# Retention scores from unscaled queries and keys, a block ahead, before two feed-forward layers

## Chip, cores, metric

One core of a Trainium2 chip. The metric is device time in microseconds (us) of one execution, the median of several runs. The engines are TensorE (PE, the matrix multiplies; PEld is its loading of weights), VectorE (DVE), ScalarE (ACT), GpSimd (POOL) and SyncE (SP), which here issues all transfers.

## What is computed

```python
scores = scale * np.matmul(q, k.transpose(0, 1, 3, 2))
gamma = 1.0 - 2.0 ** (-5.0 - np.arange(H, dtype=np.float32))
rel = pos[:, None] - pos[None, :]
Dmat = np.where(rel >= 0, gamma[:, None, None] ** rel[None, :, :], 0.0)
ret = np.matmul(scores * Dmat[None, :, :, :], v)
x = ret.transpose(0, 2, 1, 3).reshape(B * S, H * D)
h = x @ w_in;  x = (h * sigmoid(h)) @ w_out
h = x @ w2_in; y = (np.maximum(h, 0.0) + alpha * np.minimum(h, 0.0)) @ w2_out
```

B = 4 sequences, H = 8 heads, S = 576 positions, D = 64; 2304 tokens in all, model width 512, inner width 2048. Everything is float32.

## The kernel before

**Stages.** The tokens are 18 blocks of 128. Retention is computed block by block in chunks of 64 positions (two chunks to a block, nine to a sequence): scores between the positions of one chunk, and a running state (keys times values of the chunks before) for everything earlier. Its results, split into a high and a low part (`xhi`, `xlo`), feed the two feed-forward layers. Those run over five token tiles (256, then four of 512) and over groups of the inner width; each product is three matmuls (high times high, low times high, high times low). The weights come as 512 KB transfers into `raw` and are decoded into a high and a low part by ACT, DVE and POOL (`weight`).

**A retention block.** Each block's q, k (features in partitions) and k, v (tokens in partitions) come as two transfers of 512 KB into a pack of four slots (`att_load`): slots 0 and 1 are q and k for the scores, slots 2 and 3 are k and v for the state and the output. There are five packs, two of them in the still unused end of `sums`. `att_prep` multiplies q by a table of decay factors (`qtab`, built piece by piece by `att_table`) and v by another one, in place, on POOL or on DVE. `att_half`, called twice a block, alternates on PE eight score products (into the buffer `sc`) and eight state products (into `total`), all 64x64, and copies the state. `att_mask` multiplies the scores by a mask of ones and zeros: the decay is already in q and v. `att_out` makes the products of old state and q and of masked scores and v in the buffer `xo`, and copies out `xhi` and `xlo`. There is one `sc`, one `total` and one `xo`.

**What sets the order.** All instructions are recorded first and then ordered by a planner (`Program.order`): every engine but PE takes the ready instruction with the earliest due time; on PE there are two queues of units, "retention" and "layers", and a started unit is finished first. `DUE` gives the first two weights due times of their own. On each engine, and in SP's queue of transfers, the order that comes out is kept as it stands: an instruction that waits holds up those behind it. In `att_step(n)` block n+1 is loaded, scaled and scored while block n's output is made. Some transfers wait for a one-column copy on ACT (`gate`) that stands for an earlier transfer or result.

**Start.** 22 matmuls on a zero tile (`warm(WARM)`) run while the first data comes; the first six blocks have two more each, so 34 in all.

Names in the rows: `sums` (two packs and later the layers' sums), `pack_111` to `pack_113` (the other packs), `att` (score and state tiles, tables, masked scores), `bank` (accumulators of the layers), `low`, `top`, `a`, `w` (weight decoding). Nearly every instruction is recorded by one helper, so it carries line 280 (281 in the changed kernel).

Of the kernel before, what the change touches and what calls it, by code (L numbers as in the profile page):

```python
# [9 lines left out]
F32 = mybir.dt.float32  # L10
# [8 lines left out]
P = 128  # L19
# [7 lines left out]
C = 64  # L27
# [3 lines left out]
SIZES = [[1, 2, 3, 4, 4, 2], [4, 4, 4, 4]]  # L31
GROUPS = [(i, range(sum(sizes[:n]), sum(sizes[:n + 1]))) for i, sizes in enumerate(SIZES) for n in range(len(sizes))]
WARM, WARM_BLOCKS = 22, 6
DUE = {0: -1e5, 1: 6e3}
LATER = [5, 6, 8, 9, 11, 12]
LEAD = 4
TILES = [256, 512, 512, 512, 512]
RAWS = 2
PACKS = 5
STATES = 4  # L40
PERIOD = 2 * S // P
SMALL = [C, PERIOD * H, NPAIR * NCH, NPAIR * C]
ORDER = [0, 2, 4, 6, 1, 3, 5, 7]


# [238 lines left out]
def retention_ffn_kernel(ctx: ExitStack, tc: tile.TileContext, qkv, w1, w2, alpha, small, out):  # L284
# [37 lines left out]
            self.n += 1  # L322
            return self.tiles[(self.n - 1) % len(self.tiles)]

    rings = {k: Ring() for k in ("w0", "w1", "g", "act", "down", "pr", "state", "bank", "raw", "top", "low", "a")}
    rings["raw"].grow(big, "raw", 512, RAWS, I64)
    rings["top"].grow(big, "top", 512, 2)
    rings["low"].grow(big, "low", 512, 2)
# [12 lines left out]
    att = att_pool.enter_context(tc.tile_pool(name="att", bufs=1))  # L341
    PACK = 4 * DM
    spare = [sums[:, NC * NT - (i + 1) * PACK:NC * NT - i * PACK] for i in range(2)]
    packs = [att.tile([P, PACK], F32, name=f"pack{i}") for i in range(3)]
    packs = [spare[0], packs[0], packs[1], spare[1], packs[2]]
    sizes = 2 * [2 * NPAIR * C] + STATES * [NPAIR * D] + SMALL + [NPAIR * S]
    ends = np.cumsum([0] + sizes)
    rest = att.tile([P, int(ends[-1])], F32, name="att")
    *more, mask, vtab, fac, base, qtab = (rest[:, a:b] for a, b in zip(ends, ends[1:]))
    small_sb = rest[:, ends[-6]:ends[-2]]  # L350
    mask = mask.unsqueeze(1).unsqueeze(1).to_broadcast([P, 2, NPAIR, C])
    vtab = vtab.rearrange("p (n h) -> p n h", h=H)
    fac = fac.rearrange("p (c n) -> p c n", c=NPAIR)
    base = base.rearrange("p (c t) -> p c t", c=NPAIR)
    qtab = qtab.rearrange("p (c n t) -> p c n t", c=NPAIR, t=C)
    rings["pr"].tiles = more[:2]
    rings["state"].tiles = more[2:]

    def close_att():
        nc.issue()  # L360
# [7 lines left out]
    def pack(n):  # L368
        return packs[n % PACKS].rearrange("p (s a) -> p s a", s=4)

# [55 lines left out]

    probs, states = {}, {}

    def rows(j):
        return slice(j * C, (j + 1) * C)

    def quarter(out, lhsT, rhs, start=True):
        nc.tensor.matmul(out, lhsT, rhs, start=start, stop=True, skip_group_check=True)

    def heads(n, i):
        return pack(n)[:, i].rearrange("p (h d) -> p h d", h=H)

    def pairs(n, i):  # L440
        return pack(n)[:, i].rearrange("p (c t) -> p c t", c=NPAIR)

    def att_load(n):
        if 0 < n < PACKS:
            for i in (0, 2):
                gate(pack(n)[:, i], fac[:, 0] if n == 1 else pack(n - 2)[:, i + 1])
        nc.sync.dma_start(out=pack(n)[:, 0:2], in_=qkv[n, :, 0:2])
        nc.sync.dma_start(out=pack(n)[:, 2:4], in_=qkv[n, :, 2:4])
# [5 lines left out]
    def att_prep(n):  # L454

        prep = ("gpsimd", "tensor_tensor"), ("vector", "tensor_tensor")
        q = pack(n)[:, 0].rearrange("p (c x t) -> p c x t", x=2, t=C)
        at = 2 * n % NCH
        for a, b, x in ((at, at + 2, 0),) if at + 2 <= NCH else ((at, NCH, 0), (0, 1, 1)):
            if 2 * n < NCH and a:  # L460
                att_table(a, b)
            part = q[:, :, x:x + b - a]
            nc.either(prep, out=part, in0=part, in1=qtab[:, :, a:b], op=ALU.mult)
        v = heads(n, 3)
        nc.either(prep, out=v, in0=v, in1=vtab[:, n % PERIOD].unsqueeze(2).to_broadcast([P, H, D]), op=ALU.mult)

    def att_half(n, c):

        nc.unit("retention", c == 1)
        q, k = pairs(n, 0), pairs(n, 1)  # L470
        j = 1 - c
        g = 2 * n + c
        more = (g + 1) % NCH
        k2, v2 = heads(n, 2)[rows(c)], heads(n, 3)[rows(c)]
        for p in range(NPAIR):
            for i in range(2):
                quarter(two["sc"][rows(i), j, p * C:(p + 1) * C], k[rows(j), p, rows(i)], q[rows(j), p, rows(i)])
                if more:
                    quarter(total[rows(i), p * D:(p + 1) * D], k2[:, 2 * p + i], v2[:, 2 * p + i],
                            start=g % NCH == 0 and p == 0)  # L480
        if more:
            states[g + 1] = rings["state"].next()
            nc.either(COPY, states[g + 1], total[:, 0:NPAIR * D])

    def att_mask(n):
        probs[n] = rings["pr"].next()
        nc.vector.tensor_tensor(out=probs[n].rearrange("p (j c t) -> p j c t", j=2, c=NPAIR),
                                in0=two["sc"][:, :, 0:NPAIR * C].rearrange("p j (c t) -> p j c t", c=NPAIR),
                                in1=mask, op=ALU.mult)

    def att_out(n):


        at = n * P
        t0, tn = next((a, m) for a, m in SPANS if a <= at < a + m)
        q, v = pairs(n, 0), heads(n, 3)
        xo = two["xo"][:, :, 0:2 * P]
        pr = probs.pop(n).rearrange("p (j c t) -> p j c t", j=2, c=NPAIR)
        hi, lo = (acts(x, t0, tn)[:, :, at - t0:at - t0 + P] for x in (xhi, xlo))
        begun = set()  # L500

        def mm(j, p, c, lhsT, rhs):
            half = p % 2
            quarter(xo[rows(half), j, p // 2 * P + c * C:p // 2 * P + (c + 1) * C], lhsT, rhs,
                    start=(j, half) not in begun)
            begun.add((j, half))

        nc.unit("retention", True)
        for c in range(2):
            g = 2 * n + c  # L510
            if g % NCH:
                old = states[g].rearrange("p (c d) -> p c d", c=NPAIR)
                for p0 in range(0, NPAIR, 2):
                    for j in range(2):
                        for p in (p0, p0 + 1):
                            mm(j, p, c, old[rows(j), p], q[rows(j), p, rows(c)])

        def inside(cross):
            for p0 in range(0, NPAIR, 2):
                for c in range(2):  # L520
                    j = c ^ cross
                    for p in (p0, p0 + 1):
                        mm(j, p, c, v[rows(c), 2 * p + j], pr[rows(c), j, p])

        def copy(cross):
            a, b = xo[:, :, cross * C:], hi[:, :, cross * C:]
            step = (C, -C)[cross]
            nc.either(COPY, bass.AP(tensor=b.tensor, offset=b.offset, ap=[b.ap[0], (2 * tn + step, 2), (tn, 2), (1, C)]),
                           bass.AP(tensor=a.tensor, offset=a.offset, ap=[a.ap[0], (512 + step, 2), (P, 2), (1, C)]))

        inside(0)
        copy(0)
        yield
        nc.unit("retention", True)
        inside(1)
        copy(1)
        nc.vector.tensor_tensor(out=lo.rearrange("p (j p2) t -> p j p2 t", j=2),
                                in0=xo.rearrange("p j (p2 t) -> p j p2 t", p2=2),
                                in1=f32(hi).rearrange("p (j p2) t -> p j p2 t", j=2), op=ALU.subtract)

    def att_step(n):

        m = n + 1
        out = att_out(n) if n >= 0 else iter([None])
        if m < NBLK:
            att_load(m)
            att_prep(m)
            att_half(m, 0)
            if m < WARM_BLOCKS:
                warm(1)  # L550
        next(out)
        if m < NBLK:
            att_half(m, 1)
            if m < WARM_BLOCKS:
                warm(1)
            att_mask(m)
        for _ in out:
            pass

# [89 lines left out]
    ctx.enter_context(tc.manual_schedule())  # L649
    nc.vector.memset(nalpha_sb, 0.0)  # L650
    nc.scalar.activation(nalpha_sb, nalpha_sb, AF.Sigmoid)
    nc.sync.dma_start(out=small_sb, in_=small)
    att_table(0, 2)

# [14 lines left out]
    nc.scalar.copy(zero, rings["act"].tiles[0])  # L669
    nc.unit("retention")  # L670
    warm(WARM)
    att_step(-1)
    first = [(s, u) for s in range(len(TILES)) for u in hs[s] + ys[s]]
    at = 0
# [25 lines left out]
def _tables():  # L700
    gamma = 1.0 - 2.0 ** (-5.0 - np.arange(H))
    scale = 1.0 / np.sqrt(D)
    mid = S // 2
    pairs = gamma.reshape(NPAIR, 2)
    i = np.arange(C)
    rel = i[None, :] - i[:, None]
    mask = np.tile(rel >= 0, (2, 1))
    place = (np.arange(P)[:, None] + P * np.arange(PERIOD)[None, :]) % S
    vtab = (gamma[None, None, :] ** (mid - place)[:, :, None].astype(float)).reshape(P, -1)
    mine = np.repeat(pairs.T, D, axis=0)  # L710
    fac = (mine[:, :, None] ** (C * np.arange(float(NCH)))[None, None, :]).reshape(P, -1)
    base = (scale * mine[:, :, None] ** (i - float(mid))[None, None, :]).reshape(P, -1)
    tables = [np.pad(a, ((0, 0), (0, n - a.shape[1]))) for a, n in zip((mask, vtab, fac, base), SMALL)]
    return np.ascontiguousarray(np.concatenate(tables, axis=1), dtype=np.float32)
# [40 lines left out]
```

## Time and profile before

| | us |
|---|---|
| median of 3 runs | 880.76 |
| lowest and highest | 879.07, 882.34 |
| the profiled execution | 881.32 |
| its span in the trace | 879.5 |

Times in the trace count from the span's start. A row of a timeline gives start and duration of an instruction (or of several merged ones, xN) and in brackets how long its engine had been idle before it and what released it; "issue" there means that the profile shows nothing that released it. A small 64x64 matmul leaves two records on PE, one of 128x512 leaves one.

### The profile page before, as it was taken

The page shows a single profiled execution, that of the slowest core. Times are in us where ns is not written, and L with a number is a line of the kernel's source. Part 1 is how long each engine was busy: PE and PEld are TensorE (multiplying, and loading weights), DVE is VectorE, ACT ScalarE, POOL GpSimd, SP SyncE. Part 2 cuts the span into 40 slices and gives each one's busy share as a digit, 9 for nine tenths or more (in the row PEclk, how much of TensorE's full clock was granted, in tenths as well). Part 3 has the DMA queues.
Part 4 walks back from the last instruction along what each step waited for, and adds up shares of the span by engine and source line. Part 5 has one row for each costly group of instructions (what it writes and reads, how often), then busy time and mean ns, then how long its engine had stood idle before and what let it go on. Part 6 is the DMA issues. An engine that isn't in the chain of part 4 may idle for free.

```text
span 879.5 us, 14420 instructions
## 1 busy us (share of the span) xinstructions
PE 855.5 (97%) x5966; PEld 715.1 (81%) x5966; DVE 560.7 (64%) x882; ACT 380.7 (43%) x720; POOL 129.2 (15%) x99
## 2 busy tenths in 40 slices
PE   7888999999999999999999999999999999999998
PEld 5666788888888888888888888888888888888887
DVE  5667589975943499536998622984369733954342
ACT  3345465453432255223556544763345533533340
POOL 3455121220200022101210100220003200200000
PEclk8899999999999999999999999999999999999999
DMA  7786042220200033101311000330012100101102
GB/s 272 248 275 230 3 144 74 71 72 24 97 1 1 1 96 100 44 1 48 96 49 45 4 1 1 97 97 0 1 48 97 49 0 1 49 1 48 49 25 96
DMA packets 17491, 58.32 MB, mean 66 GB/s; under 512 B 2064, under 2 KB 2448, under 8 KB 17424
## 3 DMA queue, kind: packets, MB, share of 16 engines
q1 hardware_dynamic: 17424, 57.38, 19.6%
q8 instruction: 47, 0.77, 0.3%
q14 instruction: 20, 0.16, 0.1%
HBM read 52.66 MB, written 4.72 MB: 65 GB/s over the span
## 4 chain that ended last, share of the span: by engine, by line
PE 91%; DVE 5%; issue 2%; DMA 1%; POOL 1%; SPq 0%; ACT 0%; POOLq 0%; DVEq 0%; ACTq 0%
PE bank L280 87%; PE xo L280 2%; DVE a L280 2%; PE sc L280 1%; PE total L280 1%; DMA sums<-in_qkv 1%; DVE act L280 1%; DMA pack<-in_qkv 1%; DVE att L280 0%; POOL sums L280 0%; DVE xlo L280 0%; POOL pack L280 0%; DVE top L280 0%; DVE gb L280 0%; DVE w L280 0%
## 5 line engine op out<-in xcount | busy, mean ns | idle before, releaser
L280 PE MATMUL bank<-xhi,w 128*128 128x512 f32 (+1 forms) x880 | 250.8, 370 | 0.0
L280 PEld LDWEIGHTS bank<-xhi,w 128*128 128x128 f32 x880 | 159.7, 189 | 28.1
L280 POOL TENSOR_TENSOR low<-low,top 128x512 f32<-128x512 f32 x64 | 92.9, 1458 | 595.8 <-DVE top L280 584.8
L280 DVE TENSOR_TENSOR sums<-bank,sums 128x512 f32<-128x512 f32 (+1 forms) x155 | 100.7, 651 | 98.1 <-PE bank L280 96.2
L280 PE MATMUL bank<-xlo,w 128*128 128x512 f32 (+1 forms) x440 | 162.2, 369 | 0.0
L280 ACT ACTIVATE act<-bank 128x512 f32<-128x512 f32 (+1 forms) x160 | 88.4, 553 | 122.1 <-PE bank L280 119.4
L280 PE MATMUL bank<-xhi,w0b 128*128 128x512 f32 (+1 forms) x400 | 113.2, 368 | 0.0
L280 DVE SCALAR_TENSOR_TENSOR act<-down,nalpha_sb,act 128x512 f32<-128x512 f32 (+1 forms) x80 | 58.7, 734 | 84.9 <-ACT act L280 84.3
L280 PEld LDWEIGHTS bank<-xlo,w 128*128 128x128 f32 x440 | 83.2, 189 | 13.8
L280 ACT ACTIVATE down<-bank 128x512 f32<-128x512 f32 (+1 forms) x80 | 44.4, 555 | 106.7 <-PE bank L280 106.0
L280 PEld LDWEIGHTS bank<-xhi,w0b 128*128 128x128 f32 x400 | 72.6, 189 | 12.6
L280 DVE TENSOR_TENSOR act<-bank,act 128x512 f32<-128x512 f32 (+1 forms) x80 | 50.8, 635 | 48.5 <-ACT act L280 48.4
L280 PE MATMUL bank<-xlo,w0b 128*128 128x512 f32 (+1 forms) x200 | 73.6, 368 | 0.0
L280 PE MATMUL bank<-gb,w1b 128*128 128x512 f32 (+1 forms) x292 | 67.1, 363 | 1.0 <-DVE act L280 1.0
L280 DVE TENSOR_TENSOR gb<-act,gb 128x512 fp32r<-128x512 f32 (+1 forms) x79 | 52.1, 662 | 22.8 <-ACT gb L280 22.6
L280 ACT CAST g<-act 128x512 fp32r<-128x512 f32 (+1 forms) x82 | 47.6, 581 | 39.6 <-DVE act L280 39.4
L280 PE MATMUL bank<-g,w 128*128 128x512 f32 (+1 forms) x268 | 64.4, 370 | 0.0
L280 PE MATMUL bank<-w1b,gb 128*128 128x512 f32 (+1 forms) x268 | 61.9, 380 | 0.2 <-DVE gb L280 0.2
L280 ACT CAST gb<-act 128x512 fp32r<-128x512 f32 (+1 forms) x79 | 45.2, 574 | 38.3 <-DVE act L280 38.2
L280 ACT ACTIVATE top<-raw 128x512 f32<-128x512 f32 x64 | 43.1, 674 | 41.6 <-POOL low L280 34.1
L280 PEld LDWEIGHTS bank<-gb,w1b 128*128 128x128 f32 x292 | 50.6, 189 | 9.8 <-DVE act L280 1.2
L280 PEld LDWEIGHTS bank<-w1b,gb 128*128 128x128 f32 x268 | 48.6, 188 | 10.1 <-DVE gb L280 0.6
(75 smaller groups left out, 1199.0 us busy)
## 6 DMA issues: line engine op xcount, KB each, us to landing
raw<-in_w SPq DMA_DIRECT2D x64, 512.0 KB, 3.6
pack<-in_qkv SPq DMA_DIRECT2D x22, 512.0 KB, 5.3
sums<-in_qkv SPq DMA_DIRECT2D x14, 512.0 KB, 4.4
out<-sums SPq DMA_DIRECT2D x17, 256.0 KB, 2.0
out<-sums SPq DMA_DIRECT2D x2, 128.0 KB, 1.7
att<-in_small SPq DMA_DIRECT2D x1, 214.0 KB, 3.7
alpha_sb<-in_alpha SPq DMA_DIRECT2D x1, 8.0 KB, 5.3
```

Source lines behind the costliest of these rows:

```text
L280: getattr(getattr(self.nc, name), method)(*args, **kwargs)
```

## The change

Scores are made from q and k as loaded. The decay within a chunk goes into the mask, which becomes a stored table of 512 columns (`SMALL` grows by 448 columns), so the score path needs no scaling. k in slot 2 is scaled in place of v, for the state alone; scaled q goes to a tile of its own (two of them) and serves the products with the state. `att_half` of block n now makes the scores of block n+1 beside the state of block n, so before the first block there is a call for its scores alone, with n = -1. Loads run a block earlier in the program (`att_load(m + 1)`), and block 0's is recorded first of all. There are four packs instead of five, three tiles of masked scores instead of two, and no due times of their own for the first two weights.

```diff
-DUE = {0: -1e5, 1: 6e3}
+DUE = {}
-PACKS = 5
+PACKS = 4
+QS = 2
-SMALL = [C, PERIOD * H, NPAIR * NCH, NPAIR * C]
+SMALL = [2 * NPAIR * C, PERIOD * H, NPAIR * NCH, NPAIR * C]
...
-    packs = [spare[0], packs[0], packs[1], spare[1], packs[2]]
-    sizes = 2 * [2 * NPAIR * C] + STATES * [NPAIR * D] + SMALL + [NPAIR * S]
+    packs = [spare[0], packs[0], spare[1], packs[1]]
+    sizes = (3 + QS) * [2 * NPAIR * C] + STATES * [NPAIR * D] + SMALL + [NPAIR * S]
...
-    mask = mask.unsqueeze(1).unsqueeze(1).to_broadcast([P, 2, NPAIR, C])
+    mask = mask.rearrange("p (j c t) -> p j c t", j=2, c=NPAIR)
...
     def att_prep(n):
+        k = heads(n, 2)
+        nc.either(prep, out=k, in0=k, in1=vtab[:, n % PERIOD].unsqueeze(2).to_broadcast([P, H, D]), op=ALU.mult)
         q = pack(n)[:, 0].rearrange("p (c x t) -> p c x t", x=2, t=C)
+        scaled[n] = rings["q"].next().rearrange("p (c t) -> p c t", c=NPAIR)
+        new = scaled[n].rearrange("p c (x t) -> p c x t", x=2)
...
-            part = q[:, :, x:x + b - a]
-            nc.either(prep, out=part, in0=part, in1=qtab[:, :, a:b], op=ALU.mult)
-        v = heads(n, 3)
-        nc.either(prep, out=v, in0=v, in1=vtab[:, n % PERIOD].unsqueeze(2).to_broadcast([P, H, D]), op=ALU.mult)
+            nc.either(prep, out=new[:, :, x:x + b - a], in0=q[:, :, x:x + b - a], in1=qtab[:, :, a:b], op=ALU.mult)
...
     def att_half(n, c):
...
-        more = (g + 1) % NCH
-        k2, v2 = heads(n, 2)[rows(c)], heads(n, 3)[rows(c)]
+        more = n >= 0 and (g + 1) % NCH
         for p in range(NPAIR):
             for i in range(2):
-                quarter(two["sc"][rows(i), j, p * C:(p + 1) * C], k[rows(j), p, rows(i)], q[rows(j), p, rows(i)])
+                if n + 1 < NBLK:
+                    q, k = pairs(n + 1, 0), pairs(n + 1, 1)
+                    quarter(two["sc"][rows(i), j, p * C:(p + 1) * C], k[rows(j), p, rows(i)], q[rows(j), p, rows(i)])
                 if more:
...
-        q, v = pairs(n, 0), heads(n, 3)
+        q, v = scaled.pop(n), heads(n, 3)
...
     def att_step(n):
...
-            att_load(m)
             att_prep(m)
+            if m + 1 < NBLK:
+                att_load(m + 1)
             att_half(m, 0)
...
-            att_mask(m)
+            if m + 1 < NBLK:
+                att_mask(m + 1)
...
+    att_load(0)
     nc.sync.dma_start(out=small_sb, in_=small)
...
     warm(WARM)
+    att_half(-1, 0)
+    att_half(-1, 1)
+    att_mask(0)
     att_step(-1)
...
-    mask = np.tile(rel >= 0, (2, 1))
+    decay = gamma[None, None, :] ** np.maximum(rel, 0)[:, :, None] * (scale * (rel >= 0))[:, :, None]
+    mask = np.tile(decay.reshape(C, C, NPAIR, 2).transpose(0, 3, 2, 1).reshape(C, -1), (2, 1))
```

The planner makes more of it than these lines tell. Three places in the built programs, each before and then after the change:

SP's queue at its start (`att<-in_small` is the table, `sums<-in_qkv` the two halves of block 0 and later of others, `raw` a weight):

```order
1 L280 DMA raw_69<-in_w 128x512
2 L280 DMA att<-in_small 128x428
3 L280 DMA sums<-in_qkv 128x1024 x2
4 L280 DMA pack_111<-in_qkv 128x1024 x2
5 L280 DMA pack_112<-in_qkv 128x1024 x2
6 L280 DMA sums<-in_qkv 128x1024 x2
```

```order
1 L281 DMA att<-in_small 128x876
2 L281 DMA sums<-in_qkv 128x1024 x2
3 L281 DMA raw_69<-in_w 128x512
4 L281 DMA pack_111<-in_qkv 128x1024 x2
5 L281 DMA sums<-in_qkv 128x1024 x3
6 L281 DMA pack_112<-in_qkv 128x1024
7 L281 DMA pack_111<-in_qkv 128x1024
8 L281 DMA pack_112<-in_qkv 128x1024
9 L281 DMA raw_70<-in_w 128x512
```

The first weight went from first to behind block 0, and from the fifth row on the halves of different blocks are mixed.

DVE's queue at its start (`att<-sc,att` is the mask multiply of a block, `att<-att` a piece of the decay table, `a`, `top`, `w` the first weight's steps, `w_1<-a,low` the last of them, which needs POOL's `low`):

```order
2 L280 TENSOR_TENSOR att<-att 128x4x128
3 L280 TENSOR_SCALAR a_75<-top_71 128x512
4 L280 SCALAR_TENSOR_TENSOR a_75<-top_71,a_75 128x512
5 L280 TENSOR_SCALAR top_71<-a_75 128x512
6 L280 TENSOR_TENSOR a_75<-a_75,w_0_77 128x512
7 L280 TENSOR_TENSOR att<-att 128x4x128
8 L280 TENSOR_TENSOR w_1_78<-a_75,low_73 128x512
9 L280 TENSOR_TENSOR pack_111<-pack_111,att 128x512
10 L280 TENSOR_TENSOR att<-sc,att 128x512
```

```order
2 L281 TENSOR_TENSOR att<-att 128x4x128
3 L281 TENSOR_TENSOR att<-sums,att 128x512
4 L281 TENSOR_TENSOR att<-att 128x4x128
5 L281 TENSOR_TENSOR att<-sc,att 128x512
6 L281 TENSOR_SCALAR a_75<-top_71 128x512
7 L281 SCALAR_TENSOR_TENSOR a_75<-top_71,a_75 128x512
8 L281 TENSOR_SCALAR top_71<-a_75 128x512
9 L281 TENSOR_TENSOR att<-att 128x4x128
10 L281 TENSOR_TENSOR att<-sc,att 128x512
```

PE's order where retention ends (`xo` products are a block's output, `total` and `sc` state and scores, `bank` layer 1):

```order
662 L280 MATMUL xo<-att,pack_111 64x64 x8
663 L280 MATMUL sc<-pack_112 64x64 x8
664 L280 MATMUL xo<-att,pack_111 64x64 x8
665 L280 MATMUL xo<-pack_112,att 64x64 x16
666 L280 MATMUL xo<-att,pack_112 64x64 x8
667 L280 MATMUL bank_103<-g_99,w_0_85 128x512
668 L280 MATMUL bank_103<-g_99,w_1_86 128x512
669 L280 MATMUL bank_103<-g_93,w_0_85 128x512
670 L280 MATMUL xo<-att,pack_112 64x64 x8
671 L280 MATMUL bank_104<-g_99,w_0_85 128x512
```

```order
648 L281 MATMUL xo<-att,sums 64x64 x8
649 L281 MATMUL bank_103<-g_99,w_0_85 128x512
650 L281 MATMUL bank_103<-g_99,w_1_86 128x512
651 L281 MATMUL bank_103<-g_93,w_0_85 128x512
652 L281 MATMUL xo<-att,sums 64x64 x8
653 L281 MATMUL bank_104<-g_99,w_0_85 128x512
654 L281 MATMUL bank_104<-g_99,w_1_86 128x512
655 L281 MATMUL bank_104<-g_93,w_0_85 128x512
656 L281 MATMUL bank_102<-g_99,w_0_85 128x512
657 L281 MATMUL bank_102<-g_99,w_1_86 128x512
658 L281 MATMUL bank_102<-g_93,w_0_85 128x512
659 L281 MATMUL xo<-att 64x64 x16
```

Before, the outputs of the last two blocks stood next to each other; now six matmuls of layer 1 stand between them, and one pack name fewer occurs.

## Rows read from the trace of the kernel before

**Rows 1.** The page: busy time of each engine (share of the span), instructions
```profile
PE 855.5 (97%) x5966; PEld 715.1 (81%) x5966; DVE 560.7 (64%) x882; ACT 380.7 (43%) x720; POOL 129.2 (15%) x99
```

**Rows 2.** Busy time by stretch: PE, PEld, DVE, ACT, POOL, then clock, DMA share, GB/s
```profile
0.00:16.10 16.10, 9.83 (x88) 7.15 (x89) 7.91 (x11) 5.46 (x15) 6.37 (x9) 0.91 0.78 260
16.10:33.80 17.70, 14.80 (x378) 11.64 (x379) 8.58 (x14) 4.65 (x14) 5.33 (x5) 0.69 0.79 281
33.80:104.40 70.60, 60.71 (x1842) 48.33 (x1842) 49.63 (x78) 35.30 (x83) 32.70 (x27) 0.98 0.56 190
104.40:879.50 775.10, 770.15 (x3662) 647.96 (x3660) 494.61 (x781) 335.27 (x609) 84.81 (x58) 1.00 0.14 46
```

**Rows 3.** PE's waits from 0 to 105 us: total, times, longest
```profile
PE total L280 <- issue: 7.1, 7, 2.6
PE sc L280 <- issue: 4.2, 4, 2.2
PE xo L280 <- DVE xlo L280: 2.8, 4, 1.3
```

**Rows 4.** PE's timeline, single places between 0 and 104 us
```profile
2.80 6.99 PE L280 MATMUL bank<-g 128*128 128x512 f32 x22 [2.80 <-ACT g L280]
...
11.41 0.27 PE L280 MATMUL total<-sums 64*64 64x64 f32 x1 [1.13 <-POOL sums L280]
...
12.03 0.49 PE L280 MATMUL bank<-g 128*128 128x512 f32 x1
...
16.11 0.33 PE L280 MATMUL sc<-pack 64*64 64x64 f32 x1 [2.19 <-issue]
...
17.29 0.79 PE L280 MATMUL bank<-g 128*128 128x512 f32 x1
...
27.81 0.26 PE L280 MATMUL total<-sums 64*64 64x64 f32 x1 [2.58 <-issue]
...
62.79 0.27 PE L280 MATMUL total<-sums 64*64 64x64 f32 x1 [0.36 <-issue]
...
78.23 0.41 PE L280 MATMUL xo<-att,pack 64*64 64x64 f32 x16
...
87.96 0.27 PE L280 MATMUL sc<-sums 64*64 64x64 f32 x1
...
100.28 0.69 PE L280 MATMUL xo<-pack,att 64*64 64x64 f32 x32 [1.35 <-DVE xlo L280]
```

**Rows 5.** DVE's timeline, 5 to 17 us
```profile
5.94 0.69 DVE L280 SCALAR_TENSOR_TENSOR a<-top,a 128x512 int32<-128x512 int32 x1
...
10.38 1.52 DVE L280 TENSOR_TENSOR att<-att 128x512 f32<-128x512 f32 x1
13.07 1.74 DVE L280 TENSOR_TENSOR w<-a,low 128x512 fp32r<-128x512 f32 x1 [1.16 <-POOL low L280]
...
15.33 0.68 DVE L280 TENSOR_TENSOR att<-sc,att 128x512 f32<-128x512 f32 x1
```

**Rows 6.** Instruction packets, 25.3 to 26.4, then 16.1 to 104.4 us: number, MB, share
```profile
q8 instruction: 1, 0.02, 5.4%
...
q8 instruction: 18, 0.29, 1.3%
```

**Rows 7.** POOL's timeline, 8 to 15 us
```profile
12.99 1.27 POOL L280 TENSOR_TENSOR pack<-pack,att 128x512 f32<-128x512 f32 x1
```

**Rows 8.** Transfers issued at 2.1, 5.7, 25.2 us and on the page: size, us to landing
```profile
sums<-in_qkv SPq DMA_DIRECT2D x2, 512.0 KB, 7.2
...
pack<-in_qkv SPq DMA_DIRECT2D x1, 512.0 KB, 6.2
...
raw<-in_w SPq DMA_DIRECT2D x1, 512.0 KB, 7.3
...
pack<-in_qkv SPq DMA_DIRECT2D x22, 512.0 KB, 5.3
```

**Rows 9.** Busy time by stretch, 8 to 10 us (columns as in group 2)
```profile
8.00:10.00 2.00, 1.84 (x9) 1.17 (x8) 0.75 (x1) 0.71 (x2) 1.38 (x2) 1.00 1.01 385
```

More of the change, by code (lines that the diff above doesn't have):

```diff
@@ L323, in next @@
             return self.tiles[(self.n - 1) % len(self.tiles)]
-    rings = {k: Ring() for k in ("w0", "w1", "g", "act", "down", "pr", "state", "bank", "raw", "top", "low", "a")}
+    rings = {k: Ring() for k in ("w0", "w1", "g", "act", "down", "pr", "q", "state", "bank", "raw", "top", "low", "a")}
     rings["raw"].grow(big, "raw", 512, RAWS, I64)
@@ L343, in retention_ffn_kernel @@
     spare = [sums[:, NC * NT - (i + 1) * PACK:NC * NT - i * PACK] for i in range(2)]
-    packs = [att.tile([P, PACK], F32, name=f"pack{i}") for i in range(3)]
-    packs = [spare[0], packs[0], packs[1], spare[1], packs[2]]
-    sizes = 2 * [2 * NPAIR * C] + STATES * [NPAIR * D] + SMALL + [NPAIR * S]
+    packs = [att.tile([P, PACK], F32, name=f"pack{i}") for i in range(2)]
+    packs = [spare[0], packs[0], spare[1], packs[1]]
+    sizes = (3 + QS) * [2 * NPAIR * C] + STATES * [NPAIR * D] + SMALL + [NPAIR * S]
     ends = np.cumsum([0] + sizes)
@@ L355, in retention_ffn_kernel @@
     qtab = qtab.rearrange("p (c n t) -> p c n t", c=NPAIR, t=C)
-    rings["pr"].tiles = more[:2]
-    rings["state"].tiles = more[2:]
+    rings["pr"].tiles = more[:3]
+    rings["q"].tiles = more[3:3 + QS]
+    rings["state"].tiles = more[3 + QS:]
     def close_att():
@@ L422, in weight @@
         nc.due = float("inf")
-    probs, states = {}, {}
+    probs, states, scaled = {}, {}, {}
     def rows(j):
@@ L461, in att_prep @@
                 att_table(a, b)
-            part = q[:, :, x:x + b - a]
-            nc.either(prep, out=part, in0=part, in1=qtab[:, :, a:b], op=ALU.mult)
-        v = heads(n, 3)
-        nc.either(prep, out=v, in0=v, in1=vtab[:, n % PERIOD].unsqueeze(2).to_broadcast([P, H, D]), op=ALU.mult)
+            nc.either(prep, out=new[:, :, x:x + b - a], in0=q[:, :, x:x + b - a], in1=qtab[:, :, a:b], op=ALU.mult)
     def att_half(n, c):
         nc.unit("retention", c == 1)
-        q, k = pairs(n, 0), pairs(n, 1)
         j = 1 - c
         g = 2 * n + c
-        more = (g + 1) % NCH
-        k2, v2 = heads(n, 2)[rows(c)], heads(n, 3)[rows(c)]
+        more = n >= 0 and (g + 1) % NCH
         for p in range(NPAIR):
             for i in range(2):
-                quarter(two["sc"][rows(i), j, p * C:(p + 1) * C], k[rows(j), p, rows(i)], q[rows(j), p, rows(i)])
+                if n + 1 < NBLK:
+                    q, k = pairs(n + 1, 0), pairs(n + 1, 1)
+                    quarter(two["sc"][rows(i), j, p * C:(p + 1) * C], k[rows(j), p, rows(i)], q[rows(j), p, rows(i)])
                 if more:
+                    k2, v2 = heads(n, 2)[rows(c)], heads(n, 3)[rows(c)]
                     quarter(total[rows(i), p * D:(p + 1) * D], k2[:, 2 * p + i], v2[:, 2 * p + i],
```

## The prediction

> **What bounds the kernel now.** The page comes first: TensorE (PE) is busy for 97% of the span [rows 1], so the question is where the rest is. The table by stretches comes next [rows 2]. [...] All that can be won or lost lies before 104.4 us, where the retention of 18 blocks is woven into the first units of layer 1. There PE stands still for 6.3 us up to 16.1 (2.8 of them before its first instruction), for 2.9 us up to 33.8 at a mean clock of 0.69, and for 9.9 us up to 104.4. The list of PE's waits gives the causes [rows 3]: 11.3 us under "issue" (nothing that the profile shows released PE), 2.8 us for xlo. PE's own timeline [rows 4] and VectorE's (DVE) [rows 5] then show the single waits.
>
> Three of them matter.
> *The second block.* Its first scores start at 16.11, 2.19 us after PE's last work. The list calls it "issue", yet DVE shows what it was: the scores go into the one score buffer, which the mask multiply of the block before has to read first, and that ran from 15.33 to 16.01, behind the last step of a weight (13.07, after a wait for POOL) and more [rows 5].
> *The instructions themselves.* The other big "issue" gaps come inside a run of small matmuls (2.58 us before 27.81, 0.36 before 62.79) at steps of some 66 matmuls, and in the longest an instruction packet is on the way: one between 25.3 and 26.4, 18 between 16.1 and 104.4 [rows 6], against PE's 2218 matmul records and as many weight loads (each small matmul makes two of either), so about 246 records each. A packet lands late when the data queue is full.
> *The tail.* The last block's first output products wait 1.35 us for xlo of the block before [rows 4].
>
> **The change, part by part.** Off the path at no cost: the products per block stay two (q and v before, k and q now), same shapes, same engines, hidden beside PE as before; were that cover gone, one costs 1.27 us on POOL [rows 7]. The mask multiply keeps its size; its mask is a stored table instead of a broadcast one. Scaled q goes to its own tile. 288 score, 256 state and 544 output products stay, and so do the 34 warming matmuls, so the first 1,218 matmuls of PE's order are the same work in another order, and from there on the two orders agree.
>
> *Start: 1.8 us won.* SP now sends the table first, then block 0, then the first weight, then block 1. Block 1's first half stays fifth; it was issued at 5.7 and took 6.2 us, to 11.9 [rows 8]. The table has grown by 448 columns, 229 KB, which at the 385 GB/s of that moment [rows 9] is 0.6 us: 12.5. Block 0 lies ahead of the weight, so its scores (plain q and k) run at once when the warming ends at 9.8 [rows 4]. The next group (scores of block 1, state of block 0) takes 0.6 (the first group's rest ran from 11.41 to 12.03), a warming matmul 0.4, so the 57th matmul of PE's order comes at about 13.6. That place matters because, in steps of 66 back from the stall at the 188th, a block of instructions begins there. Before, the 57th came at 16.11: 2.5 won. But the mask of block 1 stands on DVE behind the first mask, three weight steps and a table piece. DVE's first piece can start about 9.8 and takes up to 1.52, the first mask 0.68: 12.0; three steps of at most 0.69, another piece and the mask [rows 5] make 16.3, when the 72nd matmul, the next score, can start. Before, the 72nd came at 17.29: 1.0 won. The gates give 1.0 and 2.5; I take the middle, 1.8, since both hold the stream. Below: nothing, if the table delays block 1 by as much as DVE gains. Above: 4.6, if block 1 lands by 10.5 because 128 longer rows of the table cost no more than 128 short ones.
>
> *The stall at 27.8: 2.2 us won.* Before, loads ran up to five blocks ahead, and around 25 us the queue was full: a weight issued at 25.2 took 7.3 us to land [rows 8]. With four packs the loads after block 5's first half wait for PE, so around that packet fewer are in flight. In lighter traffic the same kind of gap was 0.36 us [rows 4]; 2.58 less 0.36 is 2.2. Ends: nothing, and all of the 9.1 us of "issue" that is left without the 2.19 above.
>
> [...]
>
> *The tail: 1.35 us won.* Scores of the last block are done a block early, so its first output products come after six matmuls of layer 1 more, by PE's order some 1.3 us of cover, and xlo is ready. Ends: 0 and 1.35.
>
> *Added wait: the packs.* With four packs the k and v half of block b+4 is issued only when block b's output is done, and it is wanted by the state products that open the step of block b+4. The tightest such window before: block 11's output ended at 78.64, block 15 began at 87.96 [rows 4], 9.3 us. Needed: 5.3 us to land (the page's median) [rows 8], a product of 1.27 with perhaps one ahead of it on POOL [rows 7], 0.2 for the hand-overs: 8.0. It fits by 1.3 us, so I count nothing; the price if not is the slower rival's. Behind a waiting load on SP stand only loads that are wanted later.
>
> Sum: 1.8 + 2.2 + 1.35 = 5.35. The profiled execution took 881.3 us (span 879.5), 0.56 above the median of the runs, 880.76. So 881.32 less 5.35 is 875.97, and against the median **875.4 us**.
>
> **The rivals.**
> *Same time, about 878.9.* Scores no longer need scaled q, but every score still alternates on PE with a state product that needs scaled k; a step still begins when POOL is done, so in the steady part nothing is gained. If also DVE's weight steps hold the mask as before (start 0.5) and the packets are as late as before, 0.5 and 1.35 are left: 880.76 less 1.85. For it: the waits for data that are named are 2.8 us for xlo [rows 3] and 1.1 us for POOL at the start [rows 4], and next to nothing more. Against: DVE's new order has the first mask ahead of the weight.
> *Slower, about 887.4: the packs.* If landings take 7.3 us, as the slowest one shown [rows 8], the chain above needs 10.0 us against 9.3, and 14 blocks (4 to 17) are each late by 0.7: 9.8, less start and tail of 3.15, is 6.65 on top. It decides from landings of some 6.6 us. Against: these were seen only with the queue full, and after 33.8 us the other windows were 10 us and more.
> *Much faster, about 868.5.* All gaps called "issue" are data waits that go. 1.8 + 1.35 + 9.1 is 12.25, from 880.76. [...] Against: the packets in the gaps.
>
> **How the numbers follow.** What a measurement of this kernel can tell from no change is about 0.5%, 4.4 us: faster is below 876.4, slower above 885.2. The forecast gets 0.43, the same time 0.33, the slower rival 0.14, the much faster one 0.10. Faster is 0.43 + 0.10 = 0.53. The forecast stands close to the border of "faster", which is why "same" keeps a third. The range goes from 868.0, which takes in the much faster case and the upper end of the start, to 884.0, which takes in the same-time case with all gains at nothing and a few late blocks; the slower rival is left out.
>
> **What would show it.** Right: the second and third group of scores follow without a mask wait, PE's 1,218th matmul comes near 99 us instead of 104.4, the gap near 27.8 is gone or under 1 us, no 1.35 us wait before the last block's outputs, and the stretch after is as long as before. Wrong: PE waiting for POOL or DVE products of k at the start of a step from block 4 on (packs), gaps of over 2 us with an instruction packet in them, or a first group of scores that begins after 13 us.

## The result, and the profile after

The changed kernel takes **886.33 us** (median of 9 runs, 883.67 to 892.27), the kernel before 879.17 in the same session (9 runs, 875.74 to 882.34). The ratio is 1.0082, 95% interval 1.0061 to 1.0102: slower by 0.8%. The forecast was 875.4, its range 868.0 to 884.0: both missed, and on the wrong side. The profiled execution took 885.88 us, span 884.1; the one before 881.32 and 879.5.

The page shows PE as busy as before, 97%, against [rows 1]. The columns are those of that group.

```profile
PE 857.8 (97%) x5966; PEld 716.1 (81%) x5966; DVE 558.4 (63%) x878; ACT 381.7 (43%) x721; POOL 130.7 (15%) x100
```

The table by stretches of the changed kernel, with the columns of [rows 2]:

```profile
0.00:16.10 16.10, 11.29 (x125) 8.62 (x127) 6.59 (x11) 5.45 (x14) 5.46 (x9) 1.00 0.84 303
16.10:33.80 17.70, 14.76 (x458) 11.79 (x461) 11.46 (x16) 6.43 (x17) 9.60 (x9) 0.90 0.76 261
33.80:108.60 74.80, 61.45 (x1744) 47.92 (x1736) 45.21 (x72) 35.59 (x83) 30.88 (x25) 0.91 0.51 178
108.60:884.10 775.50, 770.30 (x3660) 647.77 (x3660) 495.15 (x782) 334.20 (x607) 84.75 (x58) 1.00 0.14 46
```

The last stretch is the same work in 775.5 us, before 775.1. So nearly everything happened ahead of it: the first stage ended at 104.4 and now ends at 108.6. In the first 33.8 us the changed kernel is ahead: 583 PE matmuls done against 466. At equal counts of PE's records it leads by 2.5 us at the 194th and by 4 to 6 around 40 us. It then loses some 9 to 10 us up to the end of the stage. PE's list of waits from 0 to 109 us, against [rows 3], shows where:

```profile
PE xo L281 <- issue: 6.5, 5, 2.3
PE sc L281 <- issue: 4.0, 3, 2.2
PE xo L281 <- DVE xlo L281: 3.2, 7, 0.8
...
PE total L281 <- issue: 2.1, 3, 1.4
PE sc L281 <- DVE att L281: 1.7, 2, 1.2
```

"Issue" is 12.6 us, before 11.3, of which 2.2 was the mask wait. PE's timeline gives the places that answer to [rows 4]:

```profile
12.38 0.30 PE L281 MATMUL sc<-pack 64*64 64x64 f32 x2 [0.84 <-issue]
...
15.97 0.27 PE L281 MATMUL sc<-sums 64*64 64x64 f32 x1 [1.18 <-DVE att L281]
...
29.29 0.27 PE L281 MATMUL total<-pack 64*64 64x64 f32 x2 [1.38 <-issue]
...
48.28 0.21 PE L281 MATMUL sc<-sums 64*64 64x64 f32 x1 [2.20 <-issue]
...
65.06 0.27 PE L281 MATMUL xo<-att,pack 64*64 64x64 f32 x2 [2.33 <-issue]
...
94.99 0.39 PE L281 MATMUL xo<-att,sums 64*64 64x64 f32 x10 [2.09 <-issue]
...
102.01 0.51 PE L281 MATMUL xo<-att 64*64 64x64 f32 x18 [0.43 <-DVE xlo L281]
```

The second group of scores starts at 12.38 where it started at 16.11, the third after its mask at 15.97, and the 1.35 us wait at the end is 0.43. But there are three issue gaps of over 2 us.

**What the issue gaps are.** Count PE's records in order of time: a matmul, a weight load and one of the few semaphore or drain instructions as one each. In both kernels every "issue" gap of over 0.9 us, but for the mask wait at 16.11, stands at the 194th record or a whole number of 256 behind it: the borders between blocks of PE's instructions. The page counts 47 instruction packets on q8, of 16 KB each, and the 11,983 records of PE before are 46.8 times 256. (The 0.84 us before 12.38 is at no border; it ends as the second half of block 1 lands, at 12.34.) Before: 7 borders with a gap over 0.5 us, the 706th record among them (27.81). After: 9. At nearly every one PE starts again 1.2 to 1.6 us after an instruction packet has come in. One such packet, in the DMA view from 45.9 to 47.0 us, came in 1.4 us before PE went on at 48.28:

```profile
q1 hardware_dynamic: 120, 0.43, 98.6%
q8 instruction: 1, 0.02, 5.3%
```

The packet for the next border starts only when PE has passed this one: 0.5 to 4.1 us after it at all 18 borders before, 0.7 to 5.2 us at 17 of 18 after; at the other it came 1.4 us early. SP's timeline shows what went out beside that:

```profile
48.52 0.80 SPq L281 DMA_DIRECT2D sums<-in_qkv  x2
50.33 0.33 SPq L281 DMA_DIRECT2D raw<-in_w  x1
53.86 0.33 SPq L281 DMA_DIRECT2D pack<-in_qkv  x1
```

In the DMA view from 48.3 to 53.4 us there are only data packets:

```profile
q1 hardware_dynamic: 316, 1.17, 68.9%
```

The instruction packet is in the view from 53.4 to 54.5, 5.2 us after the border:

```profile
q1 hardware_dynamic: 105, 0.39, 87.9%
q8 instruction: 1, 0.02, 5.3%
```

**The clock.** The granted clock was 0.50 for 17.07 us of the stage in both kernels. Stretches of the changed kernel, then of the one before (columns as in [rows 2]):

```profile
21.91:25.33 3.42, 3.42 (x109) 2.86 (x105) 2.50 (x4) 0.74 (x2) 1.04 (x1) 0.50 0.89 322
49.22:52.63 3.41, 3.41 (x58) 2.48 (x60) 0.86 (x3) 1.44 (x4) 0.16 (x1) 0.50 0.79 249
66.29:69.70 3.41, 3.41 (x9) 2.30 (x7) 3.27 (x5) 1.82 (x4) 1.59 (x1) 0.50 0.94 311
79.94:86.77 6.83, 6.25 (x106) 4.55 (x110) 4.41 (x9) 3.34 (x8) 4.02 (x3) 0.50 0.45 160
```

```profile
13.31:20.14 6.83, 4.63 (x99) 3.49 (x99) 4.08 (x6) 1.45 (x6) 2.33 (x3) 0.50 0.90 287
26.96:33.79 6.83, 5.98 (x119) 4.75 (x119) 1.55 (x3) 1.49 (x4) 1.27 (x1) 0.50 0.67 246
74.75:78.16 3.41, 3.41 (x80) 2.66 (x82) 0.69 (x1) 1.04 (x3) 2.15 (x2) 0.50 0.05 17
```

Before, some of this fell on waits (busy 14.0 of 17.07 us); after, on running matmuls (16.5). The stretches at 49.2 and 66.3 begin about 1 us after the gaps that end at 48.28 and 65.06; the gap that ends at 94.99 has none behind it.

**The ledger.** Take the stage as the span less the common 775.0 us, take off the gaps at borders (from one record's start to the next, where over 0.25 us, less 0.05 us that a record takes anyway: at the borders without a gap it is 0.00 to 0.05) and half of PE's busy time at 0.50. What remains is the rest: the work at full clock and all other waits.

| profiled run | stage | gaps at borders | PE busy at 0.50 | rest |
|---|---|---|---|---|
| before | 104.5 | 9.8 | 14.0 | 87.7 |
| after | 109.1 | 13.8 | 16.5 | 87.1 |

The 4.6 us are 4.0 of gaps, 1.2 of clock and 0.6 won in the rest. The ledger is that of one profiled execution each. That work at 0.50 takes twice as long is an estimate, a little high: in the changed kernel's trace a 128x512 matmul took 0.427 us from start to start at 0.50 and 0.227 at 1.00 (medians), 31 steps of small ones 0.84 and 0.46. What speaks for it is that the rest comes out alike in the runs below.

### The profile page after: what moved, and what is told of

It is laid out like the page before. It is cut to its first block, busy times and chain, and to the rows that moved or that the text cites. A ratio compares the mean times of both kernels' runs of the same rounds, so it can differ in the third digit from the quotient of the medians.

```text
span 884.1 us, 14412 instructions
## 1 busy us (share of the span) xinstructions
PE 857.8 (97%) x5966; PEld 716.1 (81%) x5966; DVE 558.4 (63%) x878; ACT 381.7 (43%) x721; POOL 130.7 (15%) x100
## 3 DMA queue, kind: packets, MB, share of 16 engines
q1 hardware_dynamic: 17424, 57.61, 19.1%
## 4 chain that ended last, share of the span: by engine, by line
PE 92%; DVE 5%; issue 2%; ACT 0%; DVEq 0%; ACTq 0%
PE bank L281 88%; PE xo L281 3%; DVE a L281 2%; PE sc L281 1%; DVE act L281 1%; DVE xlo L281 1%; PE total L281 0%; DVE att L281 0%; DVE xhi L281 0%; DVE top L281 0%; DVE gb L281 0%; ACT L281 0%; DVE g L281 0%; DVE sums L281 0%; ACT xhi L281 0%
## 5 line engine op out<-in xcount | busy, mean ns | idle before, releaser
L281 PEld LDWEIGHTS bank<-xlo,w 128*128 128x128 f32 x440 | 83.1, 189 | 14.5 <-DVE xlo L281 0.4
L281 ACT ACTIVATE down<-bank 128x512 f32<-128x512 f32 (+1 forms) x80 | 44.4, 555 | 106.7 <-PE bank L281 106.0
L281 PEld LDWEIGHTS bank<-xhi,w0b 128*128 128x128 f32 x400 | 72.6, 189 | 12.6
L281 PE MATMUL bank<-g,w 128*128 128x512 f32 (+1 forms) x268 | 67.8, 384 | 0.0
```

The source lines that it names most:

```text
L281: getattr(getattr(self.nc, name), method)(*args, **kwargs)
```

## The experiments

Theory P: four packs make the loads late. Theory O: the new order on PE and DVE. Theory F: PE's instruction packets are held up by the loads. The table at the end of this section has all runs.

**e1, e2: the packs alone.** e1 gives the changed kernel a fifth pack, e2 takes one from the kernel before.

```
-PACKS = 4
+PACKS = 5
-    packs = [spare[0], packs[0], spare[1], packs[1]]
+    packs = [spare[0], packs[0], spare[1], spare[2], packs[1]]
```

> The changed kernel with a fifth pack (a third spare one in sums), nothing else. Theory P (packs): with four packs the loads of block b+4 leave in pairs only when PE has finished block b, so they come late and meet PE's instruction packets; with five packs the lead of up to 6 us that the change has at 43 us is kept, and the time is 873 to 877 us. Theory O (order): the loss after 45 us comes from the new order of PE and DVE (scores a block ahead, no due times for weights), the packs don't matter, and it stays at 884 to 888 us.

> The kernel before with four packs instead of five, nothing else. Theory P: it loses what the change lost after its lead, some 8 to 10 us: 885 to 890 us, with PE's long issue gaps after 45 us followed by stretches at a granted clock of 0.5. Theory O: 878 to 881 us.

e1 took 887.75 us (ratio to before 1.0103, 1.0067 to 1.0138), e2 878.41 (0.9999, 0.9978 to 1.0021). P's figures fail both ways, each at one place of the borders. PE's issue waits in e1's stage are fewer (the changed kernel has seven border gaps of over 0.7 us, e1 four) but longer:

```profile
PE xo L281 <- issue: 3.8, 2, 3.3
PE sc L281 <- issue: 3.6, 1, 3.6
...
PE total L281 <- issue: 2.9, 1, 2.9
```

**e3, e4: the same order, nearly no block traffic.**

```
+            if e == "SP" and len(kwargs["out"].shape) == 3:
+                where = kwargs["out"].tensor.name, kwargs["out"].offset
+                if where in self.loaded:
+                    kwargs = {k: a[:, :, 0:8] for k, a in kwargs.items()}
+                self.loaded.add(where)
```

> The changed kernel in its own order, but from the second use of a pack on only 8 of the 512 columns of each of q, k and v are loaded (the output of those blocks is computed from the old content), so the traffic of the blocks is nearly gone. Theory F (instruction packets of PE are held up by the loads, and wait time turns into half clock): the issue gaps of 0.4 to 2.3 us after 40 us shrink to under 0.3 each, and the 1,218th matmul comes at 96 to 100 us instead of 108.6: about 875 us. Theory O: nothing but the few waits for a load goes, and it stays above 883 us.

> The kernel before in its own order with the same small loads from the second use of a pack on. Theory F: its issue gaps after 30 us (1.4, 1.1, 0.4, 1.5) go too: 873 to 876 us. Theory O: 878 to 880 us.

e3 took 871.84 us (0.9916, 0.9887 to 0.9946), e4 867.45 (a single run). Against their full-load forms that is 14.5 and 11.7 us. PE's waits in the stage of e3, then of e4:

```profile
PE xo L287 <- issue: 2.1, 3, 0.7
PE sc L287 <- issue: 1.1, 1, 1.1
PE total L287 <- issue: 0.9, 2, 0.7
...
PE bank L287 <- issue: 0.5, 1, 0.5
```

```profile
PE sc L286 <- issue: 1.0, 3, 0.4
```

In e4 no border has a gap. O falls; F holds in that the gaps shrink with the loads, from 13.8 to 5.8 us and from 9.8 to none, and was undersized: the forecasts were 875 and 873 to 876. Not expected: six of e3's gaps stayed at 0.9 to 1.3 us, where its packets still started 1.3 to 3.1 us after the border before.

**e5 to e8: move the borders.** If a gap depends on what happens to be in the queue at a border, shifting the borders against the work must change the time, with the order of the work kept. Small extra instructions at the head do that.

```
+                cut = 4 if self.warmed < FOURS else 2 if self.warmed < FOURS + TWOS else 1
+                for i in range(cut):
+                    x = slice(i * 512 // cut, (i + 1) * 512 // cut)
+                    self.nc.tensor.matmul(args[0][:, x], args[1], args[2][:, x], **kwargs)
```

> The changed kernel with ten of the first 22 warming matmuls cut into four and two into two (the same columns), which puts 32 more matmuls, 64 records, ahead of everything: the borders between PE's instruction blocks fall 64 records earlier in the work, nothing else moves. Theory G (place): where the borders fall beside the loads decides how long PE stands at each, so the sum of the gaps at the borders (13.4 us in the changed kernel, 9.5 in the one before) and with it the time moves by 2 us or more, either way, and the time follows that sum and the half-clock work to within 1.5 us. Theory S (structure): the new order of steps itself loads the queue at the wrong moments wherever the borders are: it stays at 885 to 888 us.

> The same with 64 more matmuls, 128 records, half a block: theory G: away from 886 by 2 us or more, either way, and not the same as with 64. Theory S: 885 to 888 us.

> The kernel before with the borders 64 records earlier in the work. Theory G: away from 879 by 2 us or more, either way; 879 would then be no property of its order. Theory S: 877.5 to 880.5 us.

> The kernel before with the borders 128 records earlier in the work. Theory G: away from 879 by 2 us or more, either way. Theory S: 877.5 to 880.5 us.

Measured: 881.69, 895.52, 888.63 and 887.92 us. All four left their place, as G says. But the edit itself cost time: a quarter of a warming matmul took 0.22 us and a whole one 0.32 on average, so the warming ended 5 to 6 us later with 64 records and 11 to 12 with 128, and the rest grew with it. G's other half, that the time follows gaps and clock to within 1.5 us, did not come true here: by the ledger e5 was to take 876.3 us and e6 876.9. The gaps moved regardless: 13.8 to 8.6 and 9.2, 9.8 to 15.4 and 8.0. e5 is faster than the changed kernel although it starts 5 us later.

**e9 to e12, e15, e16: move them at less cost.** Some warming matmuls give way to small ones that are to take as long together.

```
+                if self.warmed == WARM:
+                    for x in range(SMALLS):
+                        a, b = (slice(h * C, (h + 1) * C) for h in (x & 1, x >> 1 & 1))
+                        self.nc.tensor.matmul(self.spots[x >> 1 & 1][a, 0:C], args[1].bitcast(F32)[b, a], ...
+                if self.warmed > WARM - DROP:
+                    continue
```

> The changed kernel with two of the 22 warming matmuls replaced by 34 small ones (64 columns, in four quarters of the array), so that the warming takes as long as before and the borders of PE's instruction blocks fall 64 records earlier in the work. It does without the longer warming of the cut matmuls, which held the first scores back by 5 and 11 us. Theory G (place): the sum of the gaps at borders leaves 13.8 us by 2 us or more, and the time follows: 886.3 plus the difference in that sum plus half the difference in PE work at the clock of 0.5, to within 1.5 us. Theory S (structure): 885 to 888 us.

> The same with six warming matmuls replaced by 70 small ones: borders 128 records earlier. Theory G: as for 64, with another sum. Theory S: 885 to 888 us.

> The kernel before with two warming matmuls replaced by 34 small ones: borders 64 records earlier. Theory G: the sum of the gaps leaves 9.8 us by 2 us or more (it was 15.4 with the cut matmuls at this place) and the time goes to 882 us or more. Theory S: 877.5 to 880.5 us.

> The kernel before with six warming matmuls replaced by 70 small ones: borders 128 records earlier. Theory G: the time follows the sum of the gaps and half the work at the clock of 0.5, wherever it goes, to within 1.5 us. Theory S: 877.5 to 880.5 us.

> The changed kernel with ten of the first warming matmuls replaced by 106 small ones: borders 192 records earlier, the fourth place. Both theories: between 876 and 891 us, gaps plus half the work at the clock of 0.5 plus 86 to 88 us making the stage. Theory Q: the mean over the four places lies 3 us or more above that of the kernel before.

> The kernel before at the same fourth place. Theory Q: 877 to 883 us, as at its three other places, since its loads leave one at a time. Theory G alone: anything from 876 to 891 us.

The shifts are not those named: each small float32 matmul makes two matmul records and two weight loads, so the pages count 132, 268 and 404 instructions more, which is 132, 12 and 148 within a block of 256. The labels keep the old numbers. In e9 to e12 the first scores start within 1.2 us of where they did. In e15 and e16 they start 3.8 and 5.1 us later, most of it a wait at a border that now lies in the warming itself (columns as in [rows 4]; e16's is 4.36 us):

```profile
14.37 0.26 PE L288 MATMUL bank<-g 64*64 64x64 f32 x1 [3.50 <-issue]
```

So the fourth place is no pure move. The 268 and 404 instructions also put one or two borders more into the stage. The changed kernel took 877.34 us (ratio 0.9969, 0.9949 to 0.9988), 890.55 (1.0097, 1.0063 to 1.0130) and 884.55 (1.0059, 1.0038 to 1.0081); the kernel before 879.79 (0.9998, 0.9976 to 1.0019), 881.79 (1.0012, 0.9993 to 1.0032) and 882.13 (1.0025, 0.9996 to 1.0054). The issue rows of PE's waits in e9, then in e10, are the same work in the same order:

```profile
PE xo L292 <- issue: 8.2, 7, 2.0
...
PE sc L292 <- issue: 0.8, 1, 0.8
...
PE total L292 <- issue: 0.2, 1, 0.2
```

```profile
PE total L292 <- issue: 8.2, 6, 3.9
PE xo L292 <- issue: 5.8, 3, 3.6
...
PE sc L292 <- issue: 2.2, 3, 1.3
...
PE bank L292 <- issue: 1.0, 1, 1.0
```

So theory S falls for the changed kernel: instructions at the head that do no work move it by 13.2 us, from 877.3 to 890.6. The kernel before moved by 3.0, e12 and e16 just out of S's 877.5 to 880.5, and e11, whose gaps fell by 2.7, went to 879.8 where 882 or more was expected. Most sums follow the ledger: e10 was to be 886.3 plus 5.3 of gaps less 0.2 of clock, 891.4, and took 890.6; e12 was to be 882.4 and took 881.8. e11's sum gives 879.1, measured 879.8; e15's 884.6, measured 884.6. Two miss the 1.5 us. e9's gives 881.7; its profiled run took 881.4, but that was the slowest of ten, and the median lies 4.4 below. e16's gives 884.6, its profiled run took 884.4, the median 882.1. The ledger explains the profiled execution, and those of one kernel lie up to 9 us apart.

**e13, e14, e17, e18: are pairs of loads to blame?** With q and k left as loaded, their half of a pack comes free a step earlier, and SP sends it 0.4 us behind the k and v half of the block before. Of the 26 block loads behind the first ten, 8 leave within 0.8 us of the one ahead in the changed kernel, 1 before. e13 and e14 hold the q and k load back by a copy; e17 and e18 scale q in place again.

```
+        if n >= PACKS and 2 * n - 5 in states:
+            gate(pack(n)[:, 0], states[2 * n - 5])
```

```
-        scaled[n] = rings["q"].next().rearrange("p (c t) -> p c t", c=NPAIR)
-        new = scaled[n].rearrange("p c (x t) -> p c x t", x=2)
+        scaled[n], new = pairs(n, 0), q
```

> The changed kernel with each later q and k load (from block 4 on) held until the state of half a step later has been copied (one column copied by ScalarE into the pack), so that it no longer leaves 0.4 us behind the load of k and v. Theory Q (pairs of loads hold up the instruction packets): the packets start within 3 us of the border before, the sum of the gaps at borders falls from 13.8 us to under 10, and the time to 882 us or less. Theory G alone (place, whatever the loads' spacing): the sum moves either way, and the time stays within 877 to 891.

> The same held loads at the place of the borders that was worst for the changed kernel (128 records earlier, gaps 19.1 us, 890.6 us). Theory Q: the gaps fall by 5 us or more and the time to 885 us or less; with e13 the two places differ by less than the 4 us they differ by now. Theory G alone: no fall that both places show.

> The changed kernel with q scaled in place, after its scores of a block ahead, instead of into a tile of its own; scores from q and k as loaded, four packs, mask table and the order of the first loads stay. Theory Q (pairs): the gaps at borders fall from 13.8 us to 11 or less, without the waits that the copy on ScalarE brought, and the time to 882 us or less. Theory G alone: anything from 877 to 891 us.

> The same with the borders 128 records earlier, the place where the changed kernel took 890.6 us with 19.1 us of gaps. Theory Q: gaps of 15 us or less, 885 us or less, within 4 us of e17. Theory G alone: no fall that both places show.

All four have no such pair left. e13 took 884.82 us (1.0063, 1.0038 to 1.0088) with gaps of 10.9, e14 883.77 (1.0052, 1.0032 to 1.0072) with 14.9. That is half for Q: both sums fell, by 2.9 and 4.2 us, though by less than Q asked for; e14's time is under Q's 885, e13's is not under its 882; and the two places are only 1.0 us apart. e17 took 888.95 (1.0112, 1.0079 to 1.0144) with gaps of 18.0, e18 894.51 (1.0152, 1.0117 to 1.0186) with 18.1. Here no pair is left and the gaps are 4.2 us longer and 1.0 shorter than with pairs, so Q falls as the one cause; that pairs have a part in the gaps is not excluded. SP's waits from 20 to 100 us show another difference: 26 of e17's loads wait for output products, against 13 in the changed kernel, and so leave at times that PE sets. The row of the changed kernel, of e17, then of the kernel before:

```profile
SPq L281 <- PE xo L281: 36.3, 13, 5.8
```

```profile
SPq L281 <- PE xo L281: 54.0, 26, 8.0
```

```profile
SPq L280 <- PE xo L280: 46.7, 25, 5.4
```

The kernel before has nearly as many such waits, with gaps of 9.8 us. So they alone do not explain e17's 18.0, and why e17 is slow stays open.

In the table the median is that of all runs; the other columns are those of the one profiled execution, which lay 3.9 us below the median in e1 and 4.1 and 4.4 above it in e9 and e17.

| run | median us | stage | gaps at borders | PE busy at 0.50 | rest |
|---|---|---|---|---|---|
| e1 | 887.8 | 106.7 | 11.4 | 18.8 | 85.9 |
| e2 | 878.4 | 104.1 | 9.4 | 13.4 | 88.0 |
| e3 | 871.8 | 94.9 | 5.8 | 3.4 | 87.4 |
| e4 | 867.5 | 90.7 | 0 | 6.4 | 87.5 |
| e5, e6 | 881.7, 895.5 | 104.5, 115.0 | 8.6, 9.2 | 6.8, 6.8 | 92.5, 102.4 |
| e7, e8 | 888.6, 887.9 | 110.2, 110.3 | 15.4, 8.0 | 6.8, 3.4 | 91.4, 100.6 |
| e9, e10, e15 | 877.3, 890.6, 884.6 | 104.6, 113.5, 107.3 | 9.3, 19.1, 11.3 | 16.1, 16.1, 18.1 | 87.2, 86.3, 87.0 |
| e11, e12, e16 | 879.8, 881.8, 882.1 | 105.0, 105.8, 107.6 | 7.1, 14.9, 13.5 | 19.2, 10.3, 17.4 | 88.3, 85.7, 85.4 |
| e13, e14 | 884.8, 883.8 | 109.3, 109.9 | 10.9, 14.9 | 19.8, 13.3 | 88.5, 88.3 |
| e17, e18 | 889.0, 894.5 | 116.5, 118.0 | 18.0, 18.1 | 23.4, 27.9 | 86.8, 86.0 |

In all kernels but e5 to e8, whose warming was lengthened, the rest stays between 85.4 and 88.5 us, while gaps and clock make stages of 90.7 to 118.0.

**What stays open.** Over its four places the changed kernel averages 884.7 us, the kernel before 880.7. The 4.0 us between them are over the 3 that Q named beforehand. But with a spread of 13 us over four places, two of which (132 and 148) are 16 instructions and 7.2 us apart, that doesn't settle whether the change by itself lengthens the gaps. Of the packs, e1 and e2 show no loss, each at one place; the pairs are not the one cause. The scores a block ahead, the due times and the order of the first loads were not tried one by one: with the borders moving under each edit, a single run of each would not tell.

**A version that beats both.** e9 is faster than the changed kernel by 1% and than the kernel before, 880.19 beside it, by 0.3%. That lies below 0.5%, and hangs on a place that the next edit will move.

## Why the prediction was wrong

*The step that failed* is "The stall at 27.8: 2.2 us won", with its reason, "around that packet fewer are in flight". It took one border for a place of its own. There are 17 from the second on to the end of the stage, each with a packet that can be late. Their gaps went from 9.8 to 13.8 us: plus 4.0 where the term said minus 2.2. Its two ends, nothing and a gain of 9.1, left no room for a loss. But the loads were moved, not lessened, and moved loads can meet a packet as well as miss it.

At that one border, the 706th record, the gap did go; PE's timeline (columns as in [rows 4]) has no idle time there:

```profile
24.60 0.71 PE L281 MATMUL xo<-att,pack 64*64 64x64 f32 x16
```

But it went not for the reason given. 0.8 us after the border ahead of it four loads were on the way, where it had been three, and still the packet started 1.6 us after that border, before 3.7. As far as the runs show, that is luck. On average a packet does start later with more loads on the way, 0.99 us after the border with none and 3.35 with four (last section); at a single border it need not.

*A term that was missing* is the clock: work at 0.50 grew from 14.0 to 16.5 us, worth 1.2. The prediction read the 0.69 of the second stretch and gave it no price.

*Start: 1.8 us won.* Mostly right in mechanism: the first scores begin at 10.56, not at 9.8, and the third group still waited 1.18 us for its mask; but the scores' second group came 3.7 us earlier, the third at 15.97 where 16.3 was reckoned, and the 194th record 2.5 earlier. Block 1's first half landed at 11.10 where 12.5 was reckoned; the longer table, first in the queue, took 3.3 us from issue to landing, the shorter one, behind a weight, 3.7. *Tail: 1.35 won.* Mostly right: 0.43 is left at that place, and 0.62 appeared behind it, where a layer matmul waits for xhi at 108.57. But the rest of the ledger fell only 0.6, not the 3.15 of both. PE's idle time outside the borders did fall, from 9.3 to 7.3 us; its work, counted at the full clock, rose by 1.3, for the same instructions. Such differences are within the scatter of the rest.

*The packs, counted at nothing.* Right: no wait of PE for products of k in the list, and e2 shows no cost. The 0.2 us for the hand-overs fits the trace of before, in which POOL started 0.14 us after the landing it waited for (median of 12) and PE 0.05 us after POOL (median of 3). The slower rival named nearly the measured time, 887.4, by luck: nothing waits for the packs in that list, and e1, with a fifth pack, is no faster.

*Signs.* "Gaps of over 2 us with an instruction packet in them" was listed as a sign of error, and came three times. PE's 1,218th matmul, wanted near 99 us, came at 108.6. The stretch after the stage stayed as long, as said.

*The crossings.* In e4, with nearly no block traffic, no border has a gap; with full loads 7.1 to 19.1 us stand at the borders of one kernel. The prediction saw a gap of 2.58 us with an instruction packet in it, and still priced the rest of the crossings as if they would stay put.

## What to carry to other kernels

When PE runs through many small instructions while loads are under way, add up the gaps that stand at every 256th record (here 9.8 us) before changing anything, and give every edit that moves loads or instructions a range as wide as that sum, to both sides. A difference of one per cent in such a kernel says little on the edit (here the place of the borders alone moved the changed kernel by 13.2 us, 1.5%) until the same edit has been timed with the borders at a few other places. What paid here is fewer bytes in that stage: nearly all of the blocks' loads taken away gave 11.7 and 14.5 us. That is a bound, since those two kernels leave the data out.

## What the runs showed of the hardware

*How long a packet waits.* Over 272 borders of 16 kernels (all but e5 to e8), the time from passing a border to the start of the next packet grows with the loads that are issued and not yet landed shortly (0.8 us) after the border. With none it is 0.99 us on average (42 borders, no gap), with one or two 1.97 (131, gap 0.5), with three 2.95 (64, gap 1.2), with four 3.35 (30, gap 1.4). Single borders lie some 1.1 us around these means. Seven packets more started up to 1.4 us before PE's records had reached the border. The packet itself takes some 0.95 us, and where there is a gap PE goes on 1.2 to 1.6 us after it. So, by these averages, an estimate: a block of 256 records that PE gets through in under some 3.2 us would stand even with no load on the way. The shortest block without a gap took 2.84 us, in e3, where the packet started 0.27 us after the border.

With three or four loads on the way the start is some 0.6 us later for each than with none. But the trace shows when a packet starts and not when it was asked for, so whether it waits behind the loads or is asked for later is not shown.

*How sensitive that is.* 268 instructions more at the head, one block and 12, with the order of the work kept, took the changed kernel's gaps from 13.8 to 19.1 us; 132 more took them to 9.3.
